# Local attention feeding two expert layers: values' products in groups, a new beginning, and tile 0's x split chunk by chunk

## The chip, the cores and the metric

One core of a Trainium2 chip. The metric is the device time of one launch in microseconds; lower is better. Each kernel's time is the median of several runs.

## The reference

Four batches of 8 heads, 512 local and 32 global positions, head dimension 64, all float32. Global queries see all 544 keys; a local query sees the 32 global keys and the local ones within 32 positions. The heads side by side make x, 2176 rows of 512, which goes through two layers:

```python
s_ll = np.where(np.abs(pos[:, None] - pos[None, :]) <= 32, s_ll, -1e9)
a_l = sm(np.concatenate([s_lg, s_ll], axis=-1))
out_l = a_l @ concat(v_g, v_l);  out_g = sm(s_g) @ v_all
x = concat(out_g, out_l) as (B * S, H * D)
h = x @ w_in                      # 512 -> 2048
g = where(h >= 1, h, where(h <= -1, 0, (h + 1) ** 2 / 4))
x1 = g @ w_out                    # 2048 -> 512
y = ((x1 @ w_a) * (x1 @ w_b)) @ w_out2    # 512 -> 1536 -> 512
```

## The kernel before, in words

**Tiles and items.** The rows of x are cut into 17 blocks of 128 (16 local ones, and one of the global rows). Six tiles (line 44) take three blocks each, the last one block 15 and the global rows. A *local item* (`Local`, line 146) is one block with one pair of heads, so a tile of three blocks has 12 items; a *global item* (`Glob`, line 257) is a batch with half its heads, eight in all, computed while tile 4 runs. x lies transposed, as four chunks of 128 columns (one for each pair of heads) by up to 384 rows.

**An item's steps.** `load` brings queries and keys on SP's queue (line 165); `s_pe` (line 194) makes the scores of both heads, 128 by 224, in two PSUM tiles of tag "h"; `s_post` adds the mask and takes the minimum on the vector engine (line 214) and the exponentials on ScalarE (line 218), into a buffer `e` (four of them, `EBUFS`); `norm` divides by the sum (lines 222 to 225); `t_pe` transposes e on TensorE in four pieces (line 231); `t_post` copies them to `pt` on ScalarE (line 235, two buffers); `v_pe` multiplies with the values (line 241: four products of two passes each, the two heads in different halves of the array's columns); `v_post` copies the result into x's chunk (line 246).

**The order of the items** is written out in `att_atoms` (line 356): in round k come the loads, the scores of item k, the normalisation of item k-1, then (a step of its own) the transposes of item k-2, then the values' product of item k-3. Items go block by block, the four pairs of heads inside. An `att_step` runs one such step ("atom"); the main loop spreads the atoms of the next tile between the products of the tile before, by a rate that counts three atoms per item (line 824). Of the instructions of one engine the framework issues the one that is ready first by its own plan of time, roughly in the order written.

**The beginning.** The identity is made on GpSimd (line 74), the mask loaded on ScalarE's queue (line 78). Tile 0's attention runs alone, with one step of `W1` (load, conversion and split of a weight tile: lines 92, 100 to 102, 109, 110) after each eighth atom. Each of the first 12 items has a `fill` of two products of the identity with itself (line 199), which computes nothing that is used; after the last values' product of tile 0 come eight more (`bridge`, line 206). Then `x_split` (line 415) splits each chunk of x into two parts, xh on ScalarE and xl on the vector engine (lines 423, 424), and stores tile 0's parts to DRAM (line 437).

**The layers.** `h_unit` makes 128 hidden columns for a tile: for each of four chunks three products (lines 456 to 458, `hp`, tag "h", up to 384 columns), then Relu and two vector steps (lines 744 to 746). `x_unit` multiplies them with the second weight into four accumulators (`acc`, the other four PSUM banks). Units run in the order tile 0 (six units), tile 1, the rest of tile 0 (its x reloaded, line 443), tiles 2 to 5. From `ab_unit` on the second layer runs, without attention (lines 615 to 618, 681 to 683).

Of the kernel before, what the change touches and what calls it, by code (L numbers as in the profile page):

```python
# [10 lines left out]
F32 = mybir.dt.float32  # L11
F32R = mybir.dt.float32r
# [7 lines left out]
P = 128  # L20
# [28 lines left out]
NWARM, WARM_ITEMS = 2, 12  # L49
NBRIDGE = 8  # L50
FA = 6
# [6 lines left out]

EBUFS = 4


def body(tc, qk, qkd, vw, kg, vg, w1i, w1o, w2a, w2b, w2o, mask, out):
    nc = tc.nc
# [82 lines left out]
    class Local:  # L146
# [7 lines left out]
        def load(self):  # L154
            if self.stk:
                self.raw = gp["k"].tile([P, 2, P + KW], F32, name="qkd", tag="qkd", bufs=2)
                nc.sync.dma_start(self.raw, qkd[self.blk - NNAT, self.p])
            else:
                n = nat["n"] % 4
                nat["n"] += 1  # L160
                if n < 2:
                    self.qk = gp["k"].tile([P, P + KW], F32, name="qk", tag="qkd", bufs=2)
                else:
                    self.qk = gp["k"].tile([P, P + KW], F32, name="qk", tag=("kh", "kl")[n - 2], bufs=1)
                nc.sync.dma_start(self.qk, qk[self.blk, self.p])

# [12 lines left out]
        def load_v(self):  # L179
            self.v = ap.tile([KC, 2, P], F32, name="v", bufs=3)  # L180
            nc.sync.dma_start(self.v, vw[self.b, self.i, self.p])
# [19 lines left out]
        def bridge(self):  # L201

            with tc.issue_after(self.oi):
                w = ps.tile([P, 512], F32, name="bridge", tag="acc")
                for _ in range(NBRIDGE):
                    nc.tensor.matmul(w[:, :P], ident, ident, start=True, stop=True)

# [25 lines left out]
        def t_post(self):  # L233
            self.pt = ap.tile([P, 4, P], F32, name="pt", tag="pt", bufs=2)
# [12 lines left out]

# [8 lines left out]

    class Glob:
        stk = True
        t = -1
# [56 lines left out]
        def t_post(self):  # L316
            self.pt = ap.tile([P, 4, P], F32, name="ptg", tag="pt", bufs=2)
            self.pt2 = ap.tile([SG, P], F32, name="ptg2", bufs=1)
            nc.scalar.activation(self.pt, self.tp, AF.Copy)
            nc.scalar.activation(self.pt2, self.tp2, AF.Copy)  # L320
# [11 lines left out]
        def v_post(self):  # L332
            og = gp["p"].tile([P, D], F32, name="ogs", bufs=1)
            nc.vector.tensor_scalar_mul(og, self.o, self.sm[:, 0:1])
            ot = ps.tile([D, P], F32, name="ogt", tag="h")
            nc.tensor.transpose(ot, og, ident)
            t = len(TILES) - 1
            c0 = P * TILES[t].index(GLOB) + SG * self.b
            for h in range(4):
                nc.any.tensor_copy(xraw_cur[t][2 * self.q + h // 2][64 * (h % 2):64 * (h % 2) + 64, c0:c0 + SG],  # L340
                                   ot[:, 32 * h:32 * h + 32])

    items = []
# [12 lines left out]
    def att_atoms():  # L356
# [3 lines left out]
        for k in range(n + 3):  # L360
            while nl < n and nl < k + (2 if isinstance(items[nl], Glob) else 3 if items[nl].stk else 5):
                items[nl].load()
                nl += 1
            while npr < min(k + 1, nl):
                items[npr].prep()
                npr += 1
            while nv < n and nv < k + isinstance(items[nv], Glob):
                items[nv].load_v()
                nv += 1
# [45 lines left out]
    def x_split(t, W):  # L415
        hi, lo = [], []
        last = t == len(TILES) - 1
        for c in range(NC):
            pool = x5p if last else mp
            h = pool.tile([P, W if last else 384], F32R, name=f"xh{c}", bufs=1)  # L420
            l = pool.tile([P, W if last else 384], F32R, name=f"xl{c}", bufs=1)
            src = xraw_cur[t][c]
            nc.scalar.activation(h[:, :W], src[:, :W], AF.Copy)
            nc.vector.tensor_tensor(l[:, :W], src[:, :W], f32(h[:, :W]), ALU.subtract)
            hi.append(h)
            lo.append(l)
        return hi, lo

    def widths(t):
        return P * len(TILES[t])  # L430

# [45 lines left out]

    xs = {}
    acc = {}
# [187 lines left out]
    def y_block(u, j):  # L670
# [13 lines left out]
        if f == NF2 - 1:  # L684
            last = s == len(PAIRS) - 1 and j % 2
            y = mp.tile([P, 768 if last else 512], F32, name="y", tag="g" if last else "y", bufs=3 if last else 2)
            y = y[:, :512]
            if j % 2:
# [36 lines left out]
    def h_unit(t, f):  # L725
        W = widths(t)
        if t not in xs:
            xs[t] = x_split(t, W)
            if t == 0:
                x0_store()  # L730
        if (t, f) == (0, FA):
# [22 lines left out]
    def x_unit(t, f):  # L754
# [11 lines left out]
        if last:  # L766
            for e in range(NC):
                x1 = mp.tile([P, 384], F32, name="x1", tag="r", bufs=3) if e % 2 else mp.tile(
                    [P, 512], F32, name="x1", tag="y", bufs=2)
                if e % 2 or t >= nt - 2:  # L770
# [21 lines left out]
    for u in range(len(units)):  # L792
        for kind in (0, 1):
            if kind == 0:
# [26 lines left out]
                if goal[si] < nt and (u == 0 or goal[stage[u - 1]] != goal[si]):  # L821
                    n_items = ends[goal[si]] - done["n"]
                    n_units = sum(goal[i] == goal[si] for i in stage)
                    rate = 3.0 * n_items / (2 * (GLOB_END if t == nt - 2 else n_units) - 1)
                    credit = 0.0
                if (t, f) == (nt - 2, GLOB_END):
# [7 lines left out]
                    ab_load(0)  # L834
                if t == nt - 1 and f == 0:
                    xs[t] = xs_last
                h_unit(t, f)
                if (t, f) == (nt - 2, GLOB_END + 1):
                    xs_last = x_split(nt - 1, widths(nt - 1))
                if t == nt - 1:  # L840
# [72 lines left out]
def _lay(inputs):  # L913
# [21 lines left out]
    def colslices(w):  # L935
# [14 lines left out]
        "w2a": colslices(fw("moe2_w_a")), "w2b": colslices(fw("moe2_w_b")),  # L950
        "w2o": fw("moe2_w_out").reshape(NF2, P, 512), "mask": mask,
    }
# [17 lines left out]
```

## Time and profile before

| | |
|---|---|
| median of 3 runs | 939.92 us (939.34 to 940.13) |
| the profiled execution | 937.39 us |
| its span, first to last instruction | 935.6 us |
| TensorE busy | 923.4 us (99%) |
| vector engine busy | 681.6 us (73%) |
| ScalarE busy | 530.5 us (57%) |
| DMA | 114.05 MB, mean 122 GB/s |

The span is what the rows of a profile cover; the execution's own time holds 1.8 us more around it. "Idle" in front of an instruction is named with what ended it; a chain is followed back from the last instruction through what released each one. PE is TensorE's products, PEld its weight loads, DVE the vector engine, ACT ScalarE, SPq and ACTq the queues that issue transfers.

### The profile page before, as it was taken

How to read it: one execution, taken by the hardware profiler on the slowest of the kernel's cores; microseconds unless marked ns; L12 is line 12 of the kernel's file. 1: busy time of each engine (PE TensorE's matmuls, PEld its weight loads, DVE VectorE, ACT ScalarE, POOL GpSimd, SP SyncE). 2: the span in 40 equal slices, each digit the busy share in tenths (PEclk: the TensorE clock that was granted, in tenths of full speed). 3: DMA queues.
4: the chain of work that ended last, by engine and by line, in shares of the span. 5: the costliest groups of instructions: out<-in, count | busy, mean ns of one | idle time of the engine just before them, and what ended most of it. 6: DMA issues, size and time to landing. Idle time of an engine off the chain costs nothing.

```text
span 935.6 us, 16707 instructions
## 1 busy us (share of the span) xinstructions
PE 923.4 (99%) x6012; PEld 840.3 (90%) x6012; DVE 681.6 (73%) x1794; ACT 530.5 (57%) x1272; POOL 0.7 (0%) x7
## 2 busy tenths in 40 slices
PE   7999999999999999999999999999999999999997
PEld 5778999899999999987899999999999999999996
DVE  5888987678777777754359787777886666977763
ACT  7988765557666656644446455555644444654442
POOL 0000000000000000000000000000000000000000
PEclk9999999999999999999999999999999999999999
DMA  7865654766433443434464233321241111131101
GB/s 209 254 194 160 217 173 150 235 214 201 146 119 113 156 150 107 123 117 130 130 208 137 74 114 90 90 68 49 88 134 46 46 46 46 57 113 55 48 12 57
DMA packets 59299, 114.05 MB, mean 122 GB/s; under 512 B 7248, under 2 KB 28368, under 8 KB 59216
## 3 DMA queue, kind: packets, MB, share of 16 engines
q1 hardware_dynamic: 59072, 112.81, 38.5%
q8 instruction: 47, 0.77, 0.3%
q14 instruction: 36, 0.29, 0.1%
q10 hardware_dynamic: 144, 0.17, 0.1%
HBM read 95.40 MB, written 17.56 MB: 121 GB/s over the span
## 4 chain that ended last, share of the span: by engine, by line
PE 97%; DMA 1%; ACT 1%; DVE 0%; issue 0%; SPq 0%; ACTq 0%; DVEq 0%
PE acc L456 7%; PE hp L456 7%; PE acc L458 7%; PE acc L457 7%; PE hp L458 7%; PE hp L457 7%; PE pb L617 5%; PE pb L618 5%; PE pb L615 5%; PE py L682 5%; PE py L683 5%; PE py L681 5%; PE o L241 4%; PE px L618 4%; PE px L617 4%; PE px L615 4%
## 5 line engine op out<-in xcount | busy, mean ns | idle before, releaser
L456 PE MATMUL hp<-xh,w 128*128 128x384 f32 (+1 forms) x384 | 130.7, 340 | 1.2 <-DMA xh<-x0d 1.2
L456 PE MATMUL acc<-g,w 128*128 128x384 f32 (+1 forms) x384 | 131.3, 342 | 0.0
L458 PE MATMUL acc<-g,w 128*128 128x384 f32 (+1 forms) x384 | 126.4, 329 | 0.0
L457 PE MATMUL acc<-g,w 128*128 128x384 f32 (+1 forms) x384 | 126.4, 329 | 0.0
L458 PE MATMUL hp<-xl,w 128*128 128x384 f32 (+1 forms) x384 | 125.8, 328 | 0.1
L457 PE MATMUL hp<-xh,w 128*128 128x384 f32 (+1 forms) x384 | 125.3, 326 | 0.0
L109 ACT ACTIVATE w<-wt 128x512 fp32r<-128x512 f32 (+1 forms) x116 | 65.3, 564 | 67.5 <-PE pb L618 46.6
L617 PE MATMUL pb<-w 128*128 128x384 f32 (+1 forms) x288 | 94.7, 329 | 0.0
L618 PE MATMUL pb<-w 128*128 128x384 f32 (+1 forms) x288 | 94.3, 327 | 0.0
L615 PE MATMUL pb<-w 128*128 128x384 f32 (+1 forms) x288 | 93.7, 325 | 0.0
L745 DVE SCALAR_TENSOR_TENSOR m<-hp,r 128x384 f32<-128x384 f32 (+1 forms) x96 | 51.1, 532 | 56.8 <-ACT r L744 56.7
L744 ACT ACTIVATE r<-hp,half 128x384 f32<-128x384 f32 (+1 forms) x96 | 53.5, 558 | 65.2 <-PE hp L458 64.7
L682 PE MATMUL py<-w,g 128*128 128x512 f32 x204 | 80.8, 396 | 0.0
L683 PE MATMUL py<-w,g 128*128 128x512 f32 x204 | 80.7, 396 | 0.0
L681 PE MATMUL py<-w,g 128*128 128x512 f32 x204 | 79.6, 390 | 0.0
L456 PEld LDWEIGHTS hp<-xh,w 128*128 128x128 f32 x384 | 72.4, 189 | 7.8 <-issue 4.5
L456 PEld LDWEIGHTS acc<-g,w 128*128 128x128 f32 x384 | 72.4, 189 | 6.9 <-issue 5.6
L110 DVE TENSOR_TENSOR w<-wsum,w 128x256 fp32r<-128x256 f32 (+1 forms) x108 | 54.7, 508 | 31.8 <-ACT w L109 31.8
L458 PEld LDWEIGHTS acc<-g,w 128*128 128x128 f32 x384 | 72.4, 188 | 2.0 <-issue 2.0
L457 PEld LDWEIGHTS acc<-g,w 128*128 128x128 f32 x384 | 72.6, 189 | 1.0 <-issue 0.7
L110 DVE TENSOR_TENSOR w<-wt,w 128x512 fp32r<-128x512 f32 (+1 forms) x116 | 70.1, 605 | 4.1 <-ACT w L109 3.3
L458 PEld LDWEIGHTS hp<-xl,w 128*128 128x128 f32 x384 | 72.3, 188 | 0.6 <-DMA xl<-x0d 0.4
(114 smaller groups left out, 2044.2 us busy)
## 6 DMA issues: line engine op xcount, KB each, us to landing
wt<-wd SPq DMA_DIRECT2D x72, 256.0 KB, 2.7
qkd<-in_qkd_dram SPq DMA_DIRECT2D x28, 352.0 KB, 3.0
wraw<-in_w1i_dram SPq DMA_DIRECT2D x16, 512.0 KB, 3.6
wraw<-in_w1o_dram SPq DMA_DIRECT2D x16, 512.0 KB, 3.8
v<-in_vw_dram SPq DMA_DIRECT2D x64, 112.0 KB, 2.8
qk<-in_qk_dram SPq DMA_DIRECT2D x36, 176.0 KB, 3.3
wraw<-in_w2a_dram SPq DMA_DIRECT2D x12, 512.0 KB, 3.8
wraw<-in_w2b_dram SPq DMA_DIRECT2D x12, 512.0 KB, 3.9
```

The lines of the kernel that those rows point to most:

```text
L109: nc.scalar.activation(hi, src, AF.Copy)
L110: nc.vector.tensor_tensor(lo, src, f32(hi), ALU.subtract)
L456: nc.tensor.matmul(acc, whi, xhi, start=first, stop=False)
L457: nc.tensor.matmul(acc, wlo, xhi, start=False, stop=False)
L458: nc.tensor.matmul(acc, whi, xlo, start=False, stop=last)
L615: nc.tensor.matmul(out[:, :n], w[:, 0, r], hi[:, c, :n], start=start and c == 0, stop=False, skip_group_check=True)
L617: nc.tensor.matmul(out[:, :n], w[:, 1, r], hi[:, c, :n], start=False, stop=False, skip_group_check=True)
L618: nc.tensor.matmul(out[:, :n], w[:, 0, r], lo[:, c, :n], start=False, stop=k in (1, 5, 6) and c == 1, skip_group_check=True)
L681: nc.tensor.matmul(a, gh[:, c], w[:, 0], start=f == 0, stop=False)
L682: nc.tensor.matmul(a, gh[:, c], w[:, 1], start=False, stop=False)
L683: nc.tensor.matmul(a, gl[:, c], w[:, 0], start=False, stop=f == NF2 - 1)
L744: at["act"] = nc.scalar.activation(r[:, :W], hp[:, :W], AF.Relu, bias=half, scale=0.5 / W_UP).ins
```

## The change

- **Values' products in groups.** Items go pair of heads by pair of heads, the tile's blocks inside. The values' products of the (up to three) blocks of one pair are made together, into one PSUM tile 384 wide, and copied to x at once. In a round they now come ahead of the transposes, and so do the value loads, which have four buffers instead of three; `pt` has three instead of two, `e`, `mn` and `sm` three instead of four. The rate of the main loop counts two atoms per item and one per group.
- **Tile 0's x** is split chunk by chunk, each right behind its group, and the bridge goes.
- **The beginning.** The identity comes by DMA on ScalarE's queue, behind the mask and the loads of items 1 and 3. Seven items are loaded at once (three of them into buffers of `g`, which is not yet in use). The first three items have no fill; six products of a tile of zeros come before everything else.
- **Buffers that change place**: `ptg2`, `ogs`, `y` and `x1`.

```diff
-NBRIDGE = 8
+NCOLD = 3
-EBUFS = 4
+EARLY = 3
+NHEAT = 6
+EBUFS = 3
+PTBUFS = 3
+VBUFS = 4
...
-    make_identity(nc, ident)
...
-    nc.scalar.dma_start(masks, mask)
...
-                n = nat["n"] % 4
+                n = nat["n"]
                 nat["n"] += 1
-                if n < 2:
-                    self.qk = gp["k"].tile([P, P + KW], F32, name="qk", tag="qkd", bufs=2)
+                if 4 <= n < 4 + EARLY:
+                    self.qk = mp.tile([P, P + KW], F32, name="qk", tag="g", bufs=3)
                 else:
...
-                nc.sync.dma_start(self.qk, qk[self.blk, self.p])
+                    n = (n if n < 4 else n - EARLY) % 4
...
+                queue = nc.scalar if n in (1, 3) and nat["n"] <= 4 else nc.sync
+                queue.dma_start(self.qk, qk[self.blk, self.p])
...
         def v_pe(self):
-            self.o = ps.tile([P, P], F32, name="o", tag=self.tag)
-            for c in range(2):
-                for h in range(2):
-                    self.oi = nc.tensor.matmul(
-                        self.o[64 * h:64 * h + 64], self.v[:, c, 64 * h:64 * h + 64],
-                        self.pt[:KC, 2 * c + h], start=c == 0, stop=c == 1).ins
+            w = len(self.group) * P
+            self.o = ps.tile([P, w], F32, name="o", tag=self.tag)
+            for n, it in enumerate(self.group):
+                for c in range(2):
+                    for h in range(2):
+                        nc.tensor.matmul(
+                            self.o[64 * h:64 * h + 64, n * P:(n + 1) * P], it.v[:, c, 64 * h:64 * h + 64],
+                            it.pt[:KC, 2 * c + h], start=c == 0, stop=c == 1)
 
         def v_post(self):
-            nc.vector.tensor_copy(xraw_cur[self.t][self.p][:, self.j * P:(self.j + 1) * P], self.o)
+            j = self.group[0].j
+            nc.vector.tensor_copy(xraw_cur[self.t][self.p][:, j * P:(j + len(self.group)) * P], self.o)
...
+    def x_chunk(t, c, W):
...
+        nc.scalar.activation(h[:, :W], src[:, :W], AF.Copy)
+        nc.vector.tensor_tensor(l[:, :W], src[:, :W], f32(h[:, :W]), ALU.subtract)
...
-        for j, blk in enumerate(blks):
-            if blk == GLOB:
-                continue
-            for p in range(NPAIR):
-                items.append(Local(t, j, blk, p))
+        for p in range(NPAIR):
+            group = [Local(t, j, blk, p) for j, blk in enumerate(blks) if blk != GLOB]
...
-            while nl < n and nl < k + (2 if isinstance(items[nl], Glob) else 3 if items[nl].stk else 5):
+            while nl < n and nl < k + (2 if isinstance(items[nl], Glob) else 3 if items[nl].stk else 5 + EARLY * (
+                    nl < WARM_ITEMS)):
                 items[nl].load()
                 nl += 1
+                if nl == 1:
+                    nc.scalar.dma_start(masks, mask)
+                elif nl == 4:
+                    nc.scalar.dma_start(ident, eye)
...
-                if k < WARM_ITEMS:
+                if NCOLD <= k < WARM_ITEMS:
                     it.fill()
...
-            if 2 <= k <= n + 1 and items[k - 2].t is not None:
-                it = items[k - 2]
-                it.t_pe()
-                it.t_post()
-                yield k, 1
-            if 3 <= k and items[k - 3].t is not None:
+            if 3 <= k and items[k - 3].t is not None and items[k - 3].last:
                 it = items[k - 3]
...
                 it.v_pe()
                 it.v_post()
-                if k - 3 == ends[0] - 1:
-                    it.bridge()
+                if isinstance(it, Local) and it.t == 0:
+                    x_chunk(0, it.p, widths(0))
                 yield k - 3, 2
+            while nv < n and nv < k + isinstance(items[nv], Glob):
+                items[nv].load_v()
+                nv += 1
+            if 2 <= k <= n + 1 and items[k - 2].t is not None:
+                it = items[k - 2]
+                it.t_pe()
+                it.t_post()
+                yield k, 1
...
+    zero = ap.tile([P, 4, P], F32, name="zero", tag="pt", bufs=PTBUFS)
+    nc.vector.memset(zero[:, 0], 0.0)
+    w = ps.tile([P, 512], F32, name="heat", tag="acc")
+    for _ in range(NHEAT):
+        nc.tensor.matmul(w[:, :P], zero[:, 0], zero[:, 0], start=True, stop=True)
...
-                    rate = 3.0 * n_items / (2 * (GLOB_END if t == nt - 2 else n_units) - 1)
+                    n_atoms = sum(2 + it.last for it in todo)
+                    rate = n_atoms / (2.0 * (GLOB_END if t == nt - 2 else n_units) - 1)
```

## Rows read from the trace of the kernel before

**Rows 1.** The page: the span, and busy time by engine

```profile
span 935.6 us, 16707 instructions
...
PE 923.4 (99%) x6012; PEld 840.3 (90%) x6012; DVE 681.6 (73%) x1794; ACT 530.5 (57%) x1272; POOL 0.7 (0%) x7
```

**Rows 2.** TensorE's waits: engine, line, releaser, us in total, times, longest

```profile
PE s L194 <- DMA qk<-in_qk_dram: 4.0, 1, 4.0
PE s L194 <- DVE e L225: 1.2, 1, 1.2
PE hp L456 <- DMA xh<-x0d: 1.2, 1, 1.2
```

**Rows 3.** Busy time by stretch (us): length, each engine, TensorE's granted clock, DMA

```profile
5.57:8.67 3.10, 2.18 (x10) 1.45 (x8) 2.71 (x17) 1.97 (x8) 0.00 (x0) 1.00 0.98 337
15.78:38.30 22.52, 21.93 (x195) 15.77 (x194) 19.48 (x91) 22.50 (x69) 0.00 (x0) 1.00 0.75 230
...
399.00:476.00 77.00, 76.85 (x818) 62.75 (x817) 35.45 (x110) 34.30 (x104) 0.00 (x0) 1.00 0.40 125
```

**Rows 4.** The chain in the beginning: start us, us, what

```profile
0.74 3.20 DMA qk<-in_qk_dram
...
3.98 3.58 PE s L194 x15
...
9.63 1.53 PE warm L199 x12
...
14.74 0.58 PE s L194 x4
...
36.86 1.98 PE bridge L206 x16
...
41.55 0.18 PE hp L458
```

**Rows 5.** The chain in the middle, tiles 2 to 4 (two windows)

```profile
96.85 0.59 PE o L241 x8
97.44 0.37 PE acc L456
97.81 0.17 PE acc L457
...
389.69 0.59 PE o L241 x8
```

**Rows 6.** The timeline of PE and PEld: start us, us, engine, line, what

```profile
31.10 0.65 PE L194 MATMUL s<-qk 64*128 64x224 f32 x4
...
32.26 0.42 PEld L241 LDWEIGHTS o<-pt,v 112*64 112x64 f32 x8 [0.17 <-issue]
32.26 0.66 PE L241 MATMUL o<-pt,v 112*64 112x128 f32 x8
...
32.84 1.02 PE L194 MATMUL s<-qk 64*128 64x224 f32 x6
```

**Rows 7.** The timeline of ScalarE and its queue

```profile
5.57 0.48 ACT L218 ACTIVATE e<-e,mn 128x224 f32<-128x224 f32 x1 [3.12 <-DVE mn L214]
...
18.10 0.47 ACT L218 ACTIVATE e<-e,mn 128x224 f32<-128x224 f32 x1
...
19.88 0.47 ACT L224 ACTIVATE e<-e,sm 128x224 f32<-128x224 f32 x1
...
27.14 0.66 ACT L100 ACTIVATE wt<-wraw 128x512 f32<-128x512 f32 x1
...
28.23 0.47 ACT L218 ACTIVATE e<-e,mn 128x224 f32<-128x224 f32 x1
...
37.73 1.76 ACT L423 ACTIVATE xh<-xraw 128x384 fp32r<-128x384 f32 x4
```

**Rows 8.** Groups of instructions between 399 and 476 us: busy, mean ns

```profile
L301 ACT ACTIVATE eg<-sg,mng 128x272 f32<-128x272 f32 x16 | 7.6, 484 | 3.1 <-DVE mng L299 2.4 <-PE tpg L314 0.8
...
L297 DVE TENSOR_REDUCE mng<-sg 128x1 f32<-128x272 f32 x16 | 7.0, 439 | 11.1 <-PE sg L287 11.0
```

More of the change, by code (lines that the diff above doesn't have):

```diff
@@ L8 @@
 from concourse import mybir
-from concourse.masks import make_identity
 F32 = mybir.dt.float32
@@ L56, with body @@
 GLOB_END = 14
-EBUFS = 4
-def body(tc, qk, qkd, vw, kg, vg, w1i, w1o, w2a, w2b, w2o, mask, out):
+EARLY = 3
[3 more added lines that the diff above has]
+VBUFS = 4
+def body(tc, qk, qkd, vw, kg, vg, w1i, w1o, w2a, w2b, w2o, mask, eye, out):
     nc = tc.nc
@@ L158, in load @@
             else:
-                n = nat["n"] % 4
+                n = nat["n"]
                 nat["n"] += 1
-                if n < 2:
-                    self.qk = gp["k"].tile([P, P + KW], F32, name="qk", tag="qkd", bufs=2)
-                else:
-                    self.qk = gp["k"].tile([P, P + KW], F32, name="qk", tag=("kh", "kl")[n - 2], bufs=1)
-                nc.sync.dma_start(self.qk, qk[self.blk, self.p])
+                if 4 <= n < 4 + EARLY:
+                    self.qk = mp.tile([P, P + KW], F32, name="qk", tag="g", bufs=3)
+                else:
+                    n = (n if n < 4 else n - EARLY) % 4
+                    if n < 2:
+                        self.qk = gp["k"].tile([P, P + KW], F32, name="qk", tag="qkd", bufs=2)
+                    else:
+                        self.qk = gp["k"].tile([P, P + KW], F32, name="qk", tag=("kh", "kl")[n - 2], bufs=1)
+                queue = nc.scalar if n in (1, 3) and nat["n"] <= 4 else nc.sync
+                queue.dma_start(self.qk, qk[self.blk, self.p])
         def prep(self):
@@ L179, in load_v @@
         def load_v(self):
-            self.v = ap.tile([KC, 2, P], F32, name="v", bufs=3)
+            self.v = ap.tile([KC, 2, P], F32, name="v", bufs=VBUFS)
             nc.sync.dma_start(self.v, vw[self.b, self.i, self.p])
@@ L199, in fill @@
                 nc.tensor.matmul(w[:, :P], ident, ident, start=True, stop=True)
[L201 to L206, printed above, removed]
         def s_post(self):
@@ L257, in body @@
     class Glob:
+        last = True
         stk = True
@@ L316, in t_post @@
         def t_post(self):
-            self.pt = ap.tile([P, 4, P], F32, name="ptg", tag="pt", bufs=2)
-            self.pt2 = ap.tile([SG, P], F32, name="ptg2", bufs=1)
+            self.pt = ap.tile([P, 4, P], F32, name="ptg", tag="pt", bufs=PTBUFS)
+            self.pt2 = gp["k"].tile([SG, P], F32, name="ptg2", tag="qs", bufs=1)
             nc.scalar.activation(self.pt, self.tp, AF.Copy)
@@ L332, in v_post @@
         def v_post(self):
-            og = gp["p"].tile([P, D], F32, name="ogs", bufs=1)
+            og = gp["k"].tile([P, D], F32, name="ogs", tag="kh", bufs=1)
             nc.vector.tensor_scalar_mul(og, self.o, self.sm[:, 0:1])
@@ L341, in v_post, with widths @@
                                    ot[:, 32 * h:32 * h + 32])
+    xs = {}
+    def widths(t):
+        return P * len(TILES[t])
+    def x_chunk(t, c, W):
+        last = t == len(TILES) - 1
+        hi, lo = xs.setdefault(t, ([], []))
+        pool = x5p if last else mp
+        h = pool.tile([P, W if last else 384], F32R, name=f"xh{c}", bufs=1)
+        l = pool.tile([P, W if last else 384], F32R, name=f"xl{c}", bufs=1)
+        src = xraw_cur[t][c]
+        nc.scalar.activation(h[:, :W], src[:, :W], AF.Copy)
+        nc.vector.tensor_tensor(l[:, :W], src[:, :W], f32(h[:, :W]), ALU.subtract)
+        hi.append(h)
+        lo.append(l)
     items = []
@@ L345, in body @@
     for t, blks in enumerate(TILES):
-        for j, blk in enumerate(blks):
-            if blk == GLOB:
-                continue
-            for p in range(NPAIR):
-                items.append(Local(t, j, blk, p))
+        for p in range(NPAIR):
+            group = [Local(t, j, blk, p) for j, blk in enumerate(blks) if blk != GLOB]
+            for it in group:
+                it.group = group
+                it.last = it is group[-1]
+            items += group
         for b in GSCHED.get(t, []):
@@ L366, in att_atoms @@
                 npr += 1
-            while nv < n and nv < k + isinstance(items[nv], Glob):
-                items[nv].load_v()
-                nv += 1
             if k < n and items[k].t is not None:
@@ L415, in x_split @@
     def x_split(t, W):
-        hi, lo = [], []
-        last = t == len(TILES) - 1
         for c in range(NC):
[L419 to L430, printed above, removed]
+            x_chunk(t, c, W)
+        return xs[t]
     x0d = [dp.tile([P, 384], F32, name=f"x0d{i}") for i in range(2 * NC)]
@@ L470, in body @@
     W1 = WStream(ws1)
-    xs = {}
     acc = {}
@@ L685, in y_block @@
             last = s == len(PAIRS) - 1 and j % 2
-            y = mp.tile([P, 768 if last else 512], F32, name="y", tag="g" if last else "y", bufs=3 if last else 2)
-            y = y[:, :512]
+            if last:
+                y = mp.tile([P, 768], F32, name="y", tag="g", bufs=3)[:, :512]
+            else:
+                y = sp["p"].tile([P, 512], F32, name="y", bufs=2)
             if j % 2:
@@ L727, in h_unit @@
         if t not in xs:
-            xs[t] = x_split(t, W)
-            if t == 0:
-                x0_store()
+            x_split(t, W)
+        if (t, f) == (0, 0):
+            x0_store()
         if (t, f) == (0, FA):
@@ L768, in x_unit @@
                 x1 = mp.tile([P, 384], F32, name="x1", tag="r", bufs=3) if e % 2 else mp.tile(
-                    [P, 512], F32, name="x1", tag="y", bufs=2)
+                    [P, 384], F32, name="x1", bufs=2)
                 if e % 2 or t >= nt - 2:
@@ L821, in body @@
                 if goal[si] < nt and (u == 0 or goal[stage[u - 1]] != goal[si]):
-                    n_items = ends[goal[si]] - done["n"]
+                    todo = items[done["n"]:ends[goal[si]]]
                     n_units = sum(goal[i] == goal[si] for i in stage)
-                    rate = 3.0 * n_items / (2 * (GLOB_END if t == nt - 2 else n_units) - 1)
+                    n_atoms = sum(2 + it.last for it in todo)
+                    rate = n_atoms / (2.0 * (GLOB_END if t == nt - 2 else n_units) - 1)
                     credit = 0.0
@@ L834, in body @@
                     ab_load(0)
-                if t == nt - 1 and f == 0:
-                    xs[t] = xs_last
                 h_unit(t, f)
                 if (t, f) == (nt - 2, GLOB_END + 1):
-                    xs_last = x_split(nt - 1, widths(nt - 1))
+                    x_split(nt - 1, widths(nt - 1))
                 if t == nt - 1:
@@ L950, in _lay @@
         "w2a": colslices(fw("moe2_w_a")), "w2b": colslices(fw("moe2_w_b")),
-        "w2o": fw("moe2_w_out").reshape(NF2, P, 512), "mask": mask,
+        "w2o": fw("moe2_w_out").reshape(NF2, P, 512), "mask": mask, "eye": np.eye(P, dtype=np.float32),
     }
```

2 lines of the change are left out of this document (1 added, 1 removed).

## The prediction

> **What bounds the kernel now.** I read the page first: TensorE is busy for 923.4 us of a span of 935.6 us, 99% [rows 1]. So the time is TensorE's work plus its few waits, and the waits of that engine are short: 4.0 us for the first load, 1.2 us for the vector engine in the beginning, and 1.2 us for the reload of tile 0's x, which the change leaves as it is [rows 2]. A change can gain in two ways: less time on TensorE for the same products, or less waiting and filling in the beginning. Then the table by stage [rows 3]: from 15.78 to 38.30 us ScalarE is busy for 22.50 of 22.52 us, and TensorE for 21.93: tile 0's attention hangs on ScalarE as much as on TensorE. Where the global items run, from 399 to 476 us, TensorE is busy for 76.85 of 77.00 and ScalarE for 34.30.
>
> Last, the chain piece by piece. In the beginning it goes: the load until 3.98, score passes for 3.58 us, the wait for the vector engine, twelve fill passes of 1.53 us from 9.63 on, then rounds of scores, fill, transposes and values' products, one per item, up to 16 bridge passes of 1.98 us at 36.86; the first hidden product ends with the piece at 41.55 [rows 4]. In the middle an isolated values' product of one item takes 0.59 us, **and the dense product behind it takes 0.37 us where the others take 0.17** [rows 5].
>
> **Grouping the values' products.** The number of passes stays: 8 per item. What goes is the price of changing between kinds of work. A pass over 128 columns of the full array takes (1.98 - 0.20)/16 = 0.11 us in the bridge [rows 4], with the 0.20 explained next. An item's 8 passes fill half the columns each and run two at a time, so 4 x 0.11 = 0.44; they take 0.59, hence 0.15 us to enter. The dense product behind them takes 0.37 - 0.17 = 0.20 more: the price to leave. That neighbours of one kind pay the entry once is to be seen where three score products followed each other: 6 passes took 1.02 us where the 8 passes of an item's values took 0.66, and their weight loads, 0.42 us for eight, began in the same moment as the products [rows 6]; the third score product added 1.02 - 0.65 = 0.37 (0.65 for an item's four by the same view, [rows 6]), without an entry.
>
> Tiles 1 to 4 have 4 x 4 = 16 groups of three items. Two entries in three go: 32 x 0.15 = 4.8 us. In tiles 2 to 4, 36 items from 96.85 to 389.69 us, each one is followed by a dense product that pays the 0.20 [rows 5]; 12 groups pay it 12 times, so 24 x 0.20 = 4.8 us go. In tile 1 most of them are followed by scores, which pay their own entry whatever stands ahead, so I count nothing there (0.8 us at most, four exits). **Sum: 9.6 us**, all of it on the path, since but for the reload TensorE waits for nothing there [rows 2]. Tile 0's groups save TensorE some 1.2 us of entries, counted at nothing because ScalarE binds there [rows 3]; tile 5's groups have one item each and don't change. Three copies out of PSUM become one of three times the width, off the path.
>
> *A rule that speaks against it.* The rows show eight weight loads of 0.42 us beside eight products of 0.66 us, from the same start [rows 6]. The Trainium skill (TensorE: Matmul & The Clock Gate, "Part 3: Packing small matmuls") says that a weight load overlaps products in flight only where it goes to another row group. Both halves of this product use the same 112 rows, so by that rule every load would stand in the open, nothing would be saved inside a group, and the time would be that of rival (2) instead of the forecast's; the row disagrees as far as it goes.
>
> **The beginning.** (a) The bridge goes, 1.98 us of the chain [rows 4]. It covered the time from the last values' product to the first split chunk of x. Now chunks 0 to 2 are split before tile 0's last group, and 9 dense passes over them (9 x 0.17 = 1.5 us, [rows 5]) cover the copy and the split of chunk 3; if that cover fails, up to those 1.98 us come back. (b) The fills of the first three items go, 1.53 us [rows 4], and with six products of zeros ahead of the data TensorE may run at its full rate when the first item comes. Now the first 15 score passes take 3.58 us, 0.24 each, against 0.58 us for four, 0.145 each [rows 4]; the granted clock stands at 1.00 there (2.4 GHz) [rows 3], but these durations are of a slower engine, nearer to the 1.2 GHz level. The zeros cost 12 passes of at most 2 x 0.11 us = 2.6 us, under the cover of the load that ends at 3.98 [rows 4] if they begin before 1.4. (c) Of the wait of 1.2 us on the vector engine [rows 2] a part goes: with three buffers for e instead of four, item 3's minimum stands behind the first transposes, so the first norm comes earlier. (b) and (c) together are worth nothing at the least, because ScalarE has no slack from 15.78 on, and 1.53 + 1.2 = 2.7 us at the most. Between 5.57 and 8.67 ScalarE was idle for 3.10 - 1.97 = 1.1 us [rows 3]; that, and 0.3 us of an earlier first exponential (an item's four passes at 0.24 instead of 0.145), is what an earlier start can win: 1.4 us. (d) ScalarE's own sum up to the last chunk: an item takes 19.88 - 18.10 = 1.78 us, a weight conversion 28.23 - 27.14 = 1.09, the four splits 1.76 [rows 7]. The steps of tile 0 fall from 40 to 31 (15 scores, 13 transposes, 12 products; then 15, 12 and 4), so three conversions come in it instead of four (-1.1), but three more splits stand ahead of the last (+1.3): nothing in sum. **Sum: 1.98 + 1.4 = 3.4 us**, between nothing and 5.8 (1.98 + 2.7, and 1.1 if the three splits hide).
>
> (e) The loads. Items 0, 2, 4, 5, 6 stay on SP's queue, items 1 and 3 go with the mask and the identity on ScalarE's, four issues ahead of its first exponential at 5.57 [rows 7], which they would delay only from 1.2 us each on (4.8 us from the first at 0.74, [rows 4]); the first item shares the engines with the mask as before, so 3.98 stays, give or take some tenths. The identity, last on that queue, must land before the first transposes, which now come behind the fills, at 9.63 + 1.53 = 11.16 [rows 4]. The value loads move behind the groups: with four buffers the load of every third item waits on SP's queue for the group just ahead of it, with the next scores' and weights' loads behind it. Those are fetched three items ahead or more, so I cost it at nothing; without that cover up to a load's 3.20 us [rows 4] would come back at a group. The other buffers that change place (y, x1, ptg2, ogs) have no wait in the rows and are costed at nothing.
>
> Total: 9.6 + 3.4 = 13.0 us. The profiled execution took 937.39 us, so it would take 924.4; the median of the runs shown, 939.92 us, lies 2.5 us over it, and 13.0 off it gives 926.9.
>
> **The rivals.**
> (1) *The beginning gives nothing*: ScalarE holds the whole of tile 0, and the zeros change only how fast TensorE waits. For it: 22.50 of 22.52 us [rows 3]. Against: the bridge stands on the chain after ScalarE's last piece. 939.9 - 9.6 = 930.3.
> (2) *No saving inside a group*, by weight loads in the open: only the exits and the beginning are left, 4.8 + 3.4 = 8.2, so 931.7. Against it are the starts in [rows 6]. (The rule of the Trainium skill's page TensorE: Matmul & The Clock Gate, named above, would have it so.)
> (3) *The global items stall.* Now between a global item's scores and its exponentials stand the transposes two items back, because their buffers (eg has two) must come free; after the change the values' product three items back stands ahead of these, and with three buffers for sm the exponential waits for that product's scaling too. The scores hold two of the four "h" banks meanwhile, the dense product one, and the transposes want two. If TensorE waits out the chain each time (two maxima of 0.44 us and two exponentials of 0.48, 1.84 us, [rows 8]), eight items cost 14.7 us: 939.9 - 13.0 + 14.7 = 941.6. It turns the sign from 13.0/8 = 1.6 us per item on. Against: the stage has only 77.00 - 76.85 = 0.15 us of idle TensorE now [rows 3], and ScalarE is half idle, 34.30 of 77. A third of it and more, 0.7 us per item, would give 932.5.
> (4) *The zeros don't do what they are for*: the engine's rate at 3.98 is as before. Then 0.3 us is lost, 927.2, inside the forecast.
>
> **How the numbers follow.** Forecast with (4) in it: 58%, from 923 (all bounds at their best: 9.6 + 0.8 + 5.8 = 16.2, and half a microsecond of spread) to 929. (1): 15%. (2): 8%. (3) in part: 12%; in full: 7%. The range 923 to 933 takes in all but (3) in full and the tails. 0.2% is 1.9 us, about what a measurement of this kernel can tell from no change: every case but (3) in full is faster by more, so 0.92 faster, 0.02 the same, 0.06 slower.
>
> **What would show it.** In the profile after: 512 value passes in runs of 24 of some 1.45 us in the chain (12 x 0.11 + 0.15) on tiles 0 to 4, and one dense product of 0.37 behind each; if the runs take 1.77 (3 x 0.59), (2) holds. No bridge, the first hidden product finished near 38 us instead of 41.7 us [rows 4]; a score item of 0.58 us right after the load; if the first exponential starts at 5.57 as before, (4) holds. Waits of TensorE's score or transpose products on ScalarE between 400 and 476 us would be (3). Wrong would be: waits of the values' products on loads or on ScalarE after 40 us, which no row of before shows.

## The result, and the profile after

The change takes 930.05 us (median of 4 runs, 929.52 to 930.66) against 939.87 us: 9.8 us less, a ratio of 0.9896 with a 95% interval of 0.9879 to 0.9914. Timed again beside other kernels it took 930.13 us, 0.9906 (0.9888 to 0.9923). The profiled execution took 930.66 us, its span is 928.9 us.

Of the page, the span and the busy times ([rows 1] of before), and the chain's shares:

```profile
span 928.9 us, 16640 instructions
...
PE 918.3 (99%) x5996; PEld 843.4 (91%) x5996; DVE 678.5 (73%) x1755; ACT 529.5 (57%) x1272; POOL 0.3 (0%) x5
...
PE 86%; DMA 6%; DVE 4%; ACT 3%; issue 1%; ACTq 0%; SPq 0%; DVEq 0%
```

TensorE works 5.1 us less, 2.9 us of zeros included. The chain of work that ended last no longer lies on it alone: 86%, where it was 97% before.

Its waits ([rows 2] of before; engine, line, releaser, us in total, times, longest):

```profile
PE hp L470 <- DVE mn L213: 1.3, 2, 0.8
PE tp L230 <- ACT pt L234: 1.1, 1, 1.1
PE heat L722 <- DVE zero L719: 1.0, 1, 1.0
PE hp L470 <- DVE m L762: 0.8, 1, 0.8
PE s L200 <- ACT pt L234: 0.3, 1, 0.3
```

But for 0.2 us the waits for loads have gone (the zeros cover the first load, and wait 1.0 us themselves). New ones stand in their place: hidden products that wait for the minimum of scores (both use the same four PSUM banks) or for a step of the layer, transposes that wait for a copy. A group in tile 0, the last hidden products ahead of the first Relu, and a group in the middle, in the chain ([rows 5] and [rows 4]; start us, us, what):

```profile
14.18 1.02 PE o L242 x16
15.20 0.47 PE tp L230 x3
15.67 0.59 PE o L242 x8
...
41.12 0.36 PE hp L472 x2
...
147.42 1.46 PE o L242 x24
148.88 0.37 PE hp L470
149.25 0.18 PE hp L471
```

The group of 24 passes costs 1.46 us, and the dense product behind it pays the 0.37 once: both as the forecast had them. In tile 0 the third item's passes were issued behind three of the next transposes, so a group there enters twice. The group at 147.42 in the timeline, its weight loads first:

```profile
147.35 1.29 PEld L242 LDWEIGHTS o<-pt,v 112*64 112x64 f32 x24 [0.25 <-DVE sm L221]
147.35 1.53 PE L242 MATMUL o<-pt,v 112*64 112x128 f32 x24
```

The signs that the forecast named for the beginning did not all come. The bridge is gone, but the first score item took 1.12 us and not 0.58, the first exponential starts at 5.49 us (5.57 before, which was to be the sign of rival (4)), and the hidden products ahead of the first Relu end at 41.48 us, not near 38. In the timeline:

```profile
3.91 1.12 PE L200 MATMUL s<-qk 64*128 64x224 f32 x4
...
5.49 0.48 ACT L217 ACTIVATE e<-e,mn 128x224 f32<-128x224 f32 x1 [1.58 <-DVE mn L213]
```

Between 400 and 476 us TensorE waits for nothing, so rival (3) doesn't show.

### The profile page after: what moved, and what is told of

Read it like the earlier page. It is cut to its first block, busy times and chain, and to the rows that moved or that the text cites. A ratio compares the mean times of both kernels' runs of the same rounds, so it can differ in the third digit from the quotient of the medians.

```text
span 928.9 us, 16640 instructions
## 1 busy us (share of the span) xinstructions
PE 918.3 (99%) x5996; PEld 843.4 (91%) x5996; DVE 678.5 (73%) x1755; ACT 529.5 (57%) x1272; POOL 0.3 (0%) x5
## 4 chain that ended last, share of the span: by engine, by line
PE 86%; DMA 6%; DVE 4%; ACT 3%; issue 1%; ACTq 0%; SPq 0%; DVEq 0%
PE hp L470 6%; PE hp L472 6%; PE acc L470 6%; PE hp L471 6%; PE acc L471 5%; PE acc L472 5%; PE pb L627 5%; PE pb L628 5%; PE pb L625 5%; PE py L692 5%; PE py L693 5%; PE py L691 5%; PE px L625 4%; PE px L628 4%; PE px L627 4%; DMA wraw<-in_w1o_dram 3%
## 5 line engine op out<-in xcount | busy, mean ns | idle before, releaser
L766 ACT ACTIVATE g<-m 128x384 fp32r<-128x384 f32 (+1 forms) x96 | 48.5, 505 | 47.9 <-DVE m L763 45.7
```

## The experiments

Each is timed beside the kernel before on the same chip. On the three chips used that kernel's median was 939.84 us (groups alone, beginning alone, no zeros, before again), 939.67 us (change again, four weight conversions, old order, no fills) and 939.00 us (the others), so differences between kernels of different chips are uncertain by some tenths.

| kernel | median us | ratio (95% interval) |
|---|---|---|
| groups alone | 933.07 | 0.9919 (0.9900 to 0.9938) |
| beginning alone, groups of one | 942.04 | 1.0021 (1.0006 to 1.0035) |
| no zeros, first and second time | 931.39, 930.28 | 0.9902 (0.9882 to 0.9922), 0.9913 (0.9897 to 0.9928) |
| before again | 938.99 | 0.9988 (0.9972 to 1.0003) |
| change again | 930.13 | 0.9906 (0.9888 to 0.9923) |
| four weight conversions | 930.53 | 0.9908 (0.9890 to 0.9926) |
| old order for global items | 929.14 | 0.9894 (0.9874 to 0.9914) |
| no fills | 935.22 | 0.9956 (0.9939 to 0.9974) |
| old loads | 935.33 | 0.9960 (0.9945 to 0.9974) |
| one split and the bridge | 929.78 | 0.9902 (0.9886 to 0.9918) |
| old order and four conversions | 929.81 | 0.9904 (0.9889 to 0.9921) |

### Before and the change, each traced again

No edit to either.

> The kernel before unchanged, for a second trace. The profiled execution of before was 2.5 us under the median of its runs, that of the change 0.6 us over. If that is chance in when the full rate comes (7.6 us of the first score passes at half rate), this trace shows more passes at half rate and a span near 938 us; if the time lies elsewhere, the beginning is the same as before and the difference is later.

> The change unchanged, on one chip with the next three and timed in the same rounds as they: 930 us, 9 to 10 under the kernel before. It is what the next three are held against. If the time at which the full rate comes is chance, this trace has another one than 10.5 us and its beginning is moved by as much.

The second trace of before has a span of 937.6 us, nearer to the median of its runs than the first. Its chain in the beginning:

```profile
4.94 4.47 DMA qk<-in_qk_dram
...
10.66 2.57 PE warm L199 x12
```

The same work that [rows 4] show: there the twelve fills took 1.53 us, here 2.57, still at the slow rate; and TensorE waited for the fifth item's load until 9.54, a wait that the first trace doesn't have; it waits there until 8.98 for the vector engine (the timeline of TensorE; in brackets how long it stood idle before, and for what):

```profile
9.54 1.12 PE L194 MATMUL s<-qk 64*128 64x224 f32 x4 [1.80 <-DMA qk<-in_qk_dram]
```

All the 2.0 us between the two traces are lost before the first Relu of the layer, which starts at 41.83 and 43.85 us. The beginning of before varies with when a load lands and when the full rate comes; the forecast was made against a lucky execution.

With these two second traces the difference can be laid out by stretch. The Relus of the hidden products of the units 0, 6, 32, 64 and 80 of the layer (counted through all tiles) bound the stretches of the table below. They start at, in before and then in the change (the timeline of ScalarE):

```profile
43.85 0.58 ACT L744 ACTIVATE r<-hp,half 128x384 f32<-128x384 f32 x1 [0.33 <-PE hp L458]
...
90.93 0.58 ACT L744 ACTIVATE r<-hp,half 128x384 f32<-128x384 f32 x1 [1.03 <-PE hp L458]
...
222.46 0.58 ACT L744 ACTIVATE r<-hp,half 128x384 f32<-128x384 f32 x1 [1.33 <-PE hp L458]
...
396.38 0.58 ACT L744 ACTIVATE r<-hp,half 128x384 f32<-128x384 f32 x1 [2.41 <-PE hp L458]
...
491.78 0.48 ACT L744 ACTIVATE r<-hp,half 128x256 f32<-128x256 f32 x1 [1.24 <-PE hp L458]
```

```profile
40.86 0.58 ACT L761 ACTIVATE r<-hp,half 128x384 f32<-128x384 f32 x1 [0.80 <-PE hp L472]
...
87.66 0.58 ACT L761 ACTIVATE r<-hp,half 128x384 f32<-128x384 f32 x1 [1.63 <-PE hp L472]
...
216.51 0.58 ACT L761 ACTIVATE r<-hp,half 128x384 f32<-128x384 f32 x1 [2.38 <-PE hp L472]
...
385.80 0.58 ACT L761 ACTIVATE r<-hp,half 128x384 f32<-128x384 f32 x1 [1.62 <-PE hp L472]
...
483.60 0.46 ACT L761 ACTIVATE r<-hp,half 128x256 f32<-128x256 f32 x1
```

| stretch | before | change | difference | in the first two traces |
|---|---|---|---|---|
| to the first Relu | 43.85 | 40.86 | -3.0 | -0.3 |
| tile 1's attention (six units) | 47.08 | 46.80 | -0.3 | -1.3 |
| tile 2's attention (26 units) | 131.53 | 128.85 | -2.7 | -2.0 |
| tiles 3 and 4's attention (32 units) | 173.92 | 169.29 | -4.6 | -4.6 |
| tile 5's and the global items (16 units) | 95.40 | 97.80 | +2.4 | +2.2 |
| the rest | 445.83 | 444.67 | -1.2 | -0.8 |

The sum is -9.4 us, and -6.7 us between the first two traces. The last two rows belong together (+1.2, and +1.4): the change does eight more dense passes ahead of that border. So do the first two (-3.3, and -1.5), for the same reason: 20 hidden passes stand ahead of the first Relu instead of 12, some 1.4 us of work. Most of what the two pairs differ by lies in these first two rows, where before had its lucky execution.

The fourth row is the clean one. In all eleven traces with groups that stretch takes 169.21 to 169.37 us; with groups of one and everything else of the change it takes 174.11, as before.

### Groups alone

```diff
-NCOLD = 3
+NCOLD = 0
...
-EARLY = 3
-NHEAT = 6
+EARLY = 0
+NHEAT = 0
...
+    make_identity(nc, ident)
...
+    nc.scalar.dma_start(masks, mask)
...
-                queue = nc.scalar if n in (1, 3) and nat["n"] <= 4 else nc.sync
+                queue = nc.sync
...
-                if nl == 1:
-                    nc.scalar.dma_start(masks, mask)
-                elif nl == 4:
-                    nc.scalar.dma_start(ident, eye)
...
-                if isinstance(it, Local) and it.t == 0:
-                    x_chunk(0, it.p, widths(0))
+                if k - 3 == ends[0] - 1:
+                    it.bridge()
...
```

> The change with the beginning of before: identity made on GpSimd, all loads on SP's queue, fills for all twelve items, no zeros, x of tile 0 split in one go, the bridge back. Theory A (the groups carry nearly all; in the profile after, tiles 2 to 4 gained about 7 us, tile 1 nothing): 932 us, 8 under the kernel before. Theory B (the forecast's shares, 9.6 and 3.4): 930.3. Theory C (the beginning carries half): 935. In the trace TensorE's runs of 24 value passes last 1.46 us in all three.

6.8 us of the 9.8 come with the groups, between theories A and C and nearer to A. In the stretch of tile 1's attention, before (second trace), groups alone, the change (second trace), and the next experiment, groups of one (columns: length, PE, PEld, DVE, ACT, POOL busy, clock, DMA):

```profile
43.85:90.93 47.08, 47.08 (x321) 36.81 (x322) 41.55 (x144) 39.68 (x104) 0.00 (x0) 1.00 0.63 201
```

```profile
44.08:89.43 45.35, 43.34 (x317) 35.28 (x317) 41.27 (x139) 39.41 (x106) 0.00 (x0) 1.00 0.67 215
```

```profile
40.86:87.66 46.80, 44.25 (x313) 35.52 (x312) 42.20 (x138) 40.34 (x105) 0.00 (x0) 1.00 0.64 201
```

```profile
46.88:93.04 46.16, 46.15 (x322) 36.50 (x321) 41.42 (x144) 40.58 (x106) 0.00 (x0) 1.00 0.62 199
```

With groups TensorE stands idle there for 2.0 and 2.6 us, and for 1.5 in the first trace of the change; without them, in the same new order of items, for nothing. Of the 2.8 us that TensorE works less in the change than before, about half is the eight hidden passes done ahead of the border.

In both traces of the change one of these waits is 1.1 us for ScalarE's copy of a transpose. The other long one of the second trace is for a step of the layer that stands on ScalarE behind the conversion of a weight tile, and that tile's load came late (the timelines of TensorE and ScalarE):

```profile
70.92 0.66 ACT L101 ACTIVATE wt<-wraw 128x512 f32<-128x512 f32 x1 [2.20 <-DMA wraw<-in_w1o_dram]
...
72.52 0.44 PE L470 MATMUL acc<-g,w 128*128 128x384 f32 x1 [1.33 <-ACT g L766]
```

The load was issued at 65.92, when the vector engine had read the tile before it out of the buffer. So TensorE's saving turns into waits for the two other engines, and through them for a load, though neither is full: the vector engine has 42.20 of 46.80 us to do, and ScalarE stood idle for 2.20 us ahead of that conversion.

### The beginning alone

```diff
-                it.group = group
-                it.last = it is group[-1]
+                it.group = [it]
+                it.last = True
...
-                if isinstance(it, Local) and it.t == 0:
+                if isinstance(it, Local) and it.t == 0 and it.j == 2:
```

> The change with groups of one item: each item's values' product alone again, in the new order of the items; chunk splits, loads, zeros and fills as in the change. Theory A: 938 us, 2 under the kernel before, since the bridge's 2 us go and ScalarE holds the rest. Theory B: 936.5. Theory C: 935. If the new order by itself costs or gives time (other than by grouping), this and the run with groups alone will not add up to the 9.8 us of the change.

All three theories fell: 2.2 us slower than before. With groups of one the first values' product comes in round 3, not 5, and its load stands behind nine scores' loads, seven of them on the same queue; issued at 6.70, it landed 6.33 us later. TensorE's longest wait, and a stretch that begins in it:

```profile
PE o L242 <- DMA v<-in_vw_dram: 3.0, 1, 3.0
```

```profile
11.50:21.50 10.00, 8.34 (x42) 6.17 (x44) 3.92 (x18) 4.61 (x14) 0.00 (x0) 0.50 0.29 77
```

The granted clock stands at 0.50 (1.2 GHz) from that wait on to the end of the stretch. So this beginning needs the groups, which need it less (they gain 6.8 us without it), and the result of this kernel isn't the worth of the beginning.

### Old loads

```diff
-EARLY = 3
+EARLY = 0
...
-                queue = nc.scalar if n in (1, 3) and nat["n"] <= 4 else nc.sync
+                queue = nc.sync
```

> The change with the loads of before: five scores' loads ahead instead of eight, all on SP's queue; the mask and the identity stay on ScalarE's. Theory A (the loads carry nothing, since ScalarE's own work sets tile 0's end, whatever arrives early): 930 us, within 0.7 of the change. Theory B (they hide a late load: in the second trace of before TensorE waited 3.8 us for an item's load at 9.4): 1 to 3 us slower, with a wait of TensorE on a score's load between 5 and 12 us.

5.2 us slower than the change, more than theory B had. The chain, and a stretch:

```profile
3.97 1.10 PE s L200 x4
5.09 5.89 DMA qk<-in_qk_dram
11.11 1.08 PE s L200 x2
```

```profile
9.00:15.78 6.78, 4.67 (x16) 3.38 (x17) 1.30 (x7) 2.12 (x7) 0.00 (x0) 0.50 0.42 118
```

The fifth item's load can be issued only when the first item's buffer is free, at 5.09, and lands near 11; TensorE and ScalarE run dry, and the granted clock falls to 0.50. It is the late load of the second trace of before. So the new loads carry the beginning; whether by the three buffers of their own or by the second queue isn't separated, nor how much of the 5.2 us is the wait and how much the clock. The parts of the beginning don't add up: this kernel, with the old loads alone, is slower than the one with all of the old beginning (933.07 us).

### One split and the bridge

```diff
...
-                if isinstance(it, Local) and it.t == 0:
-                    x_chunk(0, it.p, widths(0))
+                if k - 3 == ends[0] - 1:
+                    it.bridge()
```

> The change with x of tile 0 split in one go behind its last group and the bridge of eight products back. The forecast's step (a): 2.0 us slower, 932, the first hidden product 2 us later. Rival (the bridge covers work that ScalarE has to do anyway): within 0.7 us of the change. More than 2 us slower would mean that the early chunks also fill waits of TensorE in tile 0.

The rival held: 929.78 us, 0.3 from the change. Its bridge stands in the chain, 1.98 us as before:

```profile
35.77 1.98 PE bridge L212 x16
```

This kernel reaches the Relu of unit 6 at 85.59 us, the change at 87.33 and 87.66. Without the bridge hidden products come earlier, but TensorE waits 1.3 us for minima in front of them, and 1.5 and 2.6 us in tile 1's stretch, where it waits 1.25 us with the bridge. What else takes the 2 us back isn't shown.

### Without the zeros, twice

```diff
...
-    zero = ap.tile([P, 4, P], F32, name="zero", tag="pt", bufs=PTBUFS)
-    nc.vector.memset(zero[:, 0], 0.0)
-    for _ in range(NHEAT):
-        nc.tensor.matmul(w[:, :P], zero[:, 0], zero[:, 0], start=True, stop=True)
```

> The change without the six products of zeros. Theory A (zeros don't bring the full rate forward: in the profile after, twelve passes of zeros took 0.21 us each and the score passes that followed still went at half rate): 930 us, within 0.7 us of the change, and the first sixteen score passes again 3.6 to 3.8 us. Theory B (they do, only later than hoped): 1 to 1.5 us slower, with the first transposes and fills at half rate, too.

> The change without the six products of zeros, a second time. Five of the six traces with zeros show the full rate by 6.1 us, the traces without them only from 8 to 13 us on. Theory A (the early rate saves TensorE time that it then spends waiting for ScalarE): 930 to 931 us. Theory B (tile 0 hangs on TensorE as well): 931.5 to 932, as in the first try's 931.4.

931.39 and 930.28 us against 930.05 and 930.13: 1.3 us the first time (theory B), and the second time nothing to be told (theory A); all four intervals overlap. Of the change's second trace and of the second without zeros, TensorE's first products of items in the timeline:

```profile
4.04 3.81 PE L200 MATMUL s<-qk 64*128 64x224 f32 x20
8.07 0.65 PE L230 MATMUL tp<-ident,e 128*112 128x128 f32 x4 [0.22 <-ACT e L223]
```

```profile
3.86 4.96 PE L200 MATMUL s<-qk 64*128 64x224 f32 x20 [3.86 <-DMA qk<-in_qk_dram]
8.75 0.91 PE L230 MATMUL tp<-ident,e 128*112 128x128 f32 x4
```

With zeros the first twenty passes took 3.81 us in that trace, without them 4.96. But in the profile after, the last sixteen alone took 3.77, and the transposes at 8.95 still took 1.03: the zeros mostly bring the full rate forward, not always. By the clock's own records the full rate is there from 4.6 to 7.1 us on in eight of the nine traces with zeros and from 10.5 us on in that one; in the five traces without them from 7.9 to 13.4 us on. Where it came early, part of the gain ended at ScalarE: TensorE was free for the first transposes at 7.85 and waited for ScalarE's norm until 8.07. At the Relu of unit 6 nothing is left of it: 86.72 and 86.86 us without zeros, 87.33 and 87.66 with them.

### No fills

```diff
-                if NCOLD <= k < WARM_ITEMS:
-                    it.fill()
```

> The change without any fill in tile 0 (nine items have one now, 4.9 us of TensorE in its profile). Theory A (ScalarE holds tile 0, as the forecast has it): no gain, within 1 us of the change, ScalarE busy throughout from 16 to 38 us. Theory B (TensorE holds it, since ScalarE has 1.5 us of slack there in the profile after): 2 to 4 us faster, 926 to 928. Theory C (the fills keep the full rate): a stretch at a granted clock of 0.5 and 2 us or more slower.

Theory C: 5.1 us slower than the change. From 5.6 to 15.78 us and from 19.2 to 36.2 us:

```profile
5.60:15.78 10.18, 8.91 (x63) 6.01 (x61) 6.58 (x37) 9.60 (x33) 0.00 (x0) 1.00 0.86 265
19.20:36.20 17.00, 16.85 (x79) 10.98 (x81) 9.08 (x40) 11.64 (x35) 0.00 (x0) 0.50 0.59 179
```

The granted clock falls to 0.50 for 17 us, and in these TensorE binds: 16.85 of 17.00 us busy, ScalarE 11.64. The ten runs agree: the one with a mean granted clock of 0.999 took 930.81 us, as the change does, and the nine at 0.985 to 0.993 took 933.8 to 938.7. So the fills of the other nine items pay for themselves.

### Four weight conversions, and the order of the global items

```diff
-START_ATOMS = 8
+START_ATOMS = 7
```

> The change with a weight conversion after every seventh step of tile 0 instead of every eighth, so that four stand ahead of the first hidden product, as before (thirty steps now give three). Theory A (the conversion pushed back is missing later: in the profile after, the chain from 54 to 137 us runs over weight loads and conversions, and TensorE waits 0.85 us at 137 and 1.1 us at 43): 1 to 1.5 us faster than the change, about 929 us, the chain back on TensorE between 90 and 137 us. Theory B (ScalarE holds tile 0): the same 1.1 us go into the beginning, and the time is that of the change, 930.

930.53 us, as the change: theory B, by time. Its profile had no wait at 137 us, but the change's second profile hadn't one either. The next run has another edit, and the one behind it has both.

```diff
+            early_t = isinstance(items[min(k, n - 1)], Glob)
+            if early_t and 2 <= k <= n + 1 and items[k - 2].t is not None:
+                it = items[k - 2]
+                it.t_pe()
+                it.t_post()
+                yield k, 1
             if 3 <= k and items[k - 3].t is not None and items[k - 3].last:
...
-            if 2 <= k <= n + 1 and items[k - 2].t is not None:
+            if not early_t and 2 <= k <= n + 1 and items[k - 2].t is not None:
```

> The change with the old order of a round (transposes, then values' product) where the round's item is a global one; everything else as in the change. In the profile after, TensorE works 1.5 us longer around tile 4's layer than before, by more single steps among the dense products, without waiting. Theory A (the order of the steps does that): 1.5 us faster than the change, 928.5. Theory B (it is the new rate of steps, or three buffers for sm): as the change, 930.

> The change with both the old order of a round for global items and a weight conversion after every seventh step. If the gains of the two profiles add up (1.4 less 0.8 us around tile 4's layer, 1.3 us in the beginning), 928.5 us; if the conversions only move a wait, 929, as with the order alone; if the order's 1.0 us was chance, 930.

929.14 and 929.81 us, 1.0 and 0.3 under the change, and the runs of all three overlap (927.66 to 931.70). No theory is told apart by these times, and no version clearly beats the change. The traces say more. Tile 5's stretch in before and the change (second traces) and with the old order for global items:

```profile
396.38:491.78 95.40, 95.25 (x930) 81.10 (x929) 47.25 (x140) 42.20 (x122) 0.00 (x0) 1.00 0.43 141
...
385.80:483.60 97.80, 97.69 (x942) 83.04 (x941) 47.11 (x141) 41.59 (x124) 0.00 (x0) 1.00 0.44 142
...
387.08:483.52 96.44, 96.21 (x934) 81.91 (x933) 49.78 (x156) 40.15 (x107) 0.00 (x0) 1.00 0.41 133
```

From the start of this stretch to the end all have the same work, but for four passes (some 0.3 us) that the new order of items leaves behind this border. For it before takes 540.9 and 541.2 us, the two traces with the old order 541.9 and 541.8, and the ten others with the new order of items 542.3 to 542.9. So the order of the steps costs about 0.6 us of the 1.2 to 1.4 us; the global items' scores, for one, keep TensorE busy for 8.96 us before and with the old order, for 9.41 in the change. Where the rest comes from stays open.

## Why the prediction was right, and where its steps failed

**The time** was forecast as 926.9 us, within 923 to 933; 930.05 us lies 3.15 above the forecast. Of the 13.0 us 9.8 came. The range also took in the case that the beginning gives nothing (930.3), so the time alone says little of the terms.

**The price of a change of work: right.** Forecast 0.15 us to enter, 0.20 to leave, 1.45 us for a group; measured 1.46 and 0.37 - 0.17. Rival (2), weight loads in the open, would have made it 1.77: 24 passes ran at the pace that two halves at a time allow, and their weight loads, 1.29 us, began in the same moment as the 1.53 us of products. The sentence of the Trainium skill (TensorE: Matmul & The Clock Gate, "Part 3: Packing small matmuls") that weight loads overlap products in flight only where the row group differs doesn't hold for these groups, which share their 112 rows; the same section also names a background weight buffer, and no run here tells whether that is at work.

**Tiles 2 to 4: 7.3 us of 8.4, and 6.6 between the first two traces.** The term (24 entries at 0.15 and 24 exits at 0.20) had one count wrong. In the order of TensorE's products 24 entries went, as forecast, but only 17 exits: 34 of the 36 values' products had a dense one behind them, not all, and in the change five more scores' products have one. 24 x 0.15 + 17 x 0.20 = 7.0 us, which is what came.

**Tile 1: the step that failed** is "all of it on the path, since but for the reload TensorE waits for nothing there". TensorE had no idle time there before (47.08 of 47.08 us); in the change it has 1.5 and 2.6 us, where 1.2 us of entries were to be won. Up to the Relu of unit 6, where both kernels have done the same layer work but for one pass, the forecast had 3.4 + 1.2 = 4.6 us, and 1.5 and 3.3 came. A TensorE that is busy for 100% beside a vector engine at 88% (41.55 of 47.08) is not one that binds alone: what it saves can become waits. That these waits come with the groups, not with the order, is shown by the two kernels that have one without the other (2.0 us and 0.01).

**Tile 5: counted at nothing, cost 1.2 us (1.4 between the first two traces).** Rival (3) named the place, but not the way: TensorE waits as little as before (76.89 of 77.00 us busy in the change's second profile), and it works longer for the same products. About half goes back with the old order of the steps. Neither of the rival's prices came.

**The beginning: the sum near (3.4 forecast; 3.0 between the kernel with groups alone and the change), its terms wrong, so that the sum is luck.** Step (a), 1.98 us for the bridge, is worth nothing: with it put back the time is the same. Step (b), the zeros, is worth at most 1.3 us, probably less; its lower bound, "ScalarE has no slack", was the better guess, and the first score item is as slow as before, as rival (4) had it. Step (e) cost the loads at nothing; without them the change is 5.2 us slower. The row that would have shown it wasn't in the one execution that the forecast read: in the second trace of before TensorE waits 1.80 us for the fifth item's load. The bound for a load that isn't covered, 3.20 us, stood in that step as a loss only, never as a gain. Rival (1), no gain in the beginning, fell by those 3.0 us, as far as the medians tell (the two ratios' intervals overlap); it forecast 930.3 us, the time that came, for another reason.

## What to carry to other kernels

Count what it costs to change between kinds of products, entry and exit, and put like ones side by side; it was worth 0.6 us for each three here where TensorE bound alone (4.6 us for the eight groups of tiles 3 and 4). Where a second engine is near 90% in the same stretch, don't count TensorE's saving in full: it can turn into waits though no other engine is full. In a beginning, look at several executions: a late load and a late full rate may be missing from the one at hand, and buffers that let loads start at once can be worth more than the work that is moved.

## What was not expected of the hardware

The full rate can be lost in the beginning and then stay away. With groups of one the granted clock fell to 0.50 within one wait of 3.0 us, and stood there for the 10 us of the stretch shown. Without fills no wait was longer than 1.1 us between the first load and the fall, TensorE worked 8.91 of the 10.18 us shown ahead of it, and the clock then stood at 0.50 for 17 us, though TensorE was busy for 16.85 us of these. The granted clock reads 1.00 from 4 to 8 us in the profile after, while sixteen score passes took 3.77 us, 0.24 each, against 0.145 each later; the durations are the better witness there.
